# An order written out by hand for the vector engines in an attention pass, with folding ahead of the normalisation

## The chip, the cores and the metric

One NeuronCore of a Trainium2 chip runs the whole program. The metric is the device time of one execution, in microseconds (us). The engines are named as in the profile: PE (TensorE; PEld is its loading of weights), ACT (ScalarE), DVE (VectorE), POOL (GpSimd) and SP (SyncE, which here only issues DMAs). Each takes its instructions in order; semaphores order them between engines.

## The reference, cut to what matters

```python
# x: (1, 2048, 640); two layers, the same weights in both
for layer in range(2):
    n = layernorm(x)
    a, b = n @ hid_re.T, n @ hid_im.T               # 640-point DFT along the channels
    x = x + (seq_re @ a - seq_im @ b)               # real part of the 2048-point DFT
    q, k, v = split_heads(layernorm(x) @ wqkv)      # 32 heads of 20 channels
    pq, pk = phi(q), phi(k)                         # phi(t) = where(t > 0, t + 1, exp(t)) + 1e-6
    kv, z = pk.T @ v, pk.sum(rows)                  # per head
    den = (pq * z).sum(channels of the head) + 1e-6
    x = x + ((pq @ kv) / den) @ wo
```

## The kernel before

The 2048 rows of x stay in SBUF as 16 tiles of 128 rows and 640 channels (X). A product in fp32 is made from two parts of each operand: a high part, rounded by ACT to TensorE's short type (fp32r), and a low part, the rest, subtracted by DVE. Three matmuls (high x high, high x low, low x high) make one product; a few are made in plain fp32, where an instruction of 512 columns counts as two in the profile.

**The attention's second pass** is the function `outputs`. M = kv times wo stands ready in five chunks (rows of M are patched into each other by small transfers). For each row tile n: POOL multiplies phi(q) by z (`weigh`, L444) three tiles ahead; DVE (`weighted`) sums this per head into denominators (L457), adds 1e-6 (L458), takes reciprocals (L459) and multiplies phi(q) by them, 600 columns (L461) and 40 columns (L467), two tiles ahead; PE transposes the weighted tile n+1 in five parts (L140); ACT and DVE split the transposed tile (L134, L135); PE multiplies it by M in 30 matmuls (L168); DVE adds the result to X[n] (L500, the residual). PSUM holds four tiles of 1024 columns, shared by transposes and products.

**Layer 1's folds** run beside it in layer 0. The 2048-point DFT uses symmetries: the channels of a normalised tile are folded (column c with column 640 - c, a sum and a difference), and the tiles of a quad a, b, c, d (tiles 4g to 4g+3) are added and subtracted: a += d, b += c, then a - b, the class "o" (odd rows), and a + b, from which classes "+" and "-" (even rows) come. Class `Fold` holds a row of stages that the loop moves on by one at each step (`tick`). For a finished tile: two passes of ACT for mean and variance (L112, L113), three small instructions of POOL (L114, L115, L118), the normalisation on ACT (L126), the channel folds on POOL (L748, L749, L753), the quad's additions on DVE and POOL (L765, L766, L774, L791), then the even ones (L808 to L812). Tiles 0 to 12 go through this (`PUSHED = 13`). The last three go through a script, the string `SECOND`, whose words each stand for one operation and its engine, followed by the rest of the folds and the splitting of DFT rows that arrive by DMA.

**What sets the order.** In `outputs` a scheduler orders each engine's instructions, with offsets by name (`AHEAD`). In the script, DVE, ACT and POOL run as written. SP's order is always as written, PE's always the scheduler's. A gate delays the script's first DMAs: they wait for the residual of tile `NT - GATE`, with NT = 16.

**After it** PE makes the class products, groups of three column blocks (L902; "cw" are plain fp32 DFT rows, "ch" and "cl" split ones), ACT and DVE split the results u (L927, L928), and the hidden DFT (L947) goes from u to the rows of x.

Of the kernel before, what the change touches and what calls it, by code (L numbers as in the profile page):

```python
# [8 lines left out]
F32 = mybir.dt.float32  # L9
F32R = mybir.dt.float32r  # L10
# [25 lines left out]
SECOND = 'w02a sda x02d x12d x03d x13d x23a sev nea dev sfv nfa dfp nda kep kdp fdp fep x32a v02v ffv kfv y23v ddv y32v a3v x22a y22v b3p c3v h3a x33a w01a v01v y33v x10a y10v l3v t3p p1v m1p P1a w00a w10a w11a v10v u20v v11v u30v u21v u22v u31v x00d x01d M1a v00p w12a v12p x11a u32v y11p Q1p N1p'  # L36
PUSHED = 13
# [5 lines left out]
PAIRS = (1, 0, 0, 0)  # L43
EVENS = (1, 1, 1, 1)
FOLDS = (0, 0)
VLOWS = (0, 0, 1, 0)
WLOWS = ((5, 2), (1, 1))
GATE = 2
# [3 lines left out]
class K:  # L52
    def __init__(self, tc, ctx):
# [10 lines left out]
        nc.vector.memset(self.mhalf, -0.5)  # L64

# [107 lines left out]
class Attention:  # L173
# [273 lines left out]
    def weighted(self, n, t1):  # L447
# [6 lines left out]
        den, rden = (  # L454
            k.sm.tile([128, H], F32, tag="sm" + n, name=k.nm(n), bufs=2) for n in ("den", "rden")
        )
# [16 lines left out]
        return t1  # L473

    def outputs(self, after, between=lambda: None):
# [4 lines left out]
        for n, i in enumerate(self.order2):  # L480
# [16 lines left out]
            for pu, hs in zip(pus, parts):  # L497
                of = lambda t: t[:, hs[0] : hs[-1] + 1, :]
                with k.ahead("res", n):
                    last = nc.vector.tensor_tensor(of(h2(X[i])), of(h2(X[i])), of(halves(pu)), op=ALU.add)  # L500
                after(i, hs[0], hs[-1] + 1)
            if n == NT - GATE:
                late = last
        return late
# [46 lines left out]
class Fold:  # L551
# [5 lines left out]
    def __init__(self, k, X, scalar):  # L557
        self.k, self.X, self.scalar, self.out, self.whole = k, X, scalar, {}, False
        self.stages = [
            self.even_low, self.even, self.odd_low, self.combine, self.pairs, self.fold, self.norm, self.stats  # L560
        ]
        self.queue = {f: [] for f in self.stages}
        self.ab, self.E, self.high, self.abcd = {}, {}, {}, {}

    def push(self, i):
        self.queue[self.stats].append((i, None))

    def tick(self):
        for n, f in enumerate(self.stages):
            todo, self.queue[f] = self.queue[f][:1], self.queue[f][1:]  # L570
            for i, v in todo:
                with self.k.ahead(f.__name__, i):
                    r = f(i, v)
                if r is not None:
                    self.queue[self.stages[n - 1]].append(r)

    def drain(self):
        while any(self.queue.values()):
            self.tick()
# [8 lines left out]
    def script(self, order, four, raws):  # L588
# [14 lines left out]
        for kind, i, c, e in order:  # L603
# [7 lines left out]
            elif kind == "s":  # L611
                xn[i] = k.temp()
                norm.setdefault(g, {})[q] = k.stats(self.X[i], xn[i] if e == "a" else None)
            elif kind == "r":
                norm[g] = self.scales(mv[g], 4 - tail[g], [i - 4 * g for i in onact if i // 4 == g])
            elif kind == "n":
                if self.whole:
                    xn[i] = k.temp()
                else:
                    self.abcd[i] = k.pqp.tile([128, D], F32, tag="pq", name=k.nm("ab"))  # L620
                k.norm(self.X[i], xn[i], norm[g][q])
            elif kind == "f":
                eng.tensor_tensor(self.abcd[i][:, 1:HD], xn[i][:, 1:HD], xn[i][:, HC:], op=ALU.add)  # L623
            elif kind == "d":
# [108 lines left out]
    def stats(self, i, _):  # L733
        k, x = self.k, self.X[i]
        xn = k.temp()
        return i, (xn, k.stats(x, xn if i in self.scalar else None))

    def norm(self, i, v):
        xn, st = v
        self.k.norm(self.X[i], xn, st)  # L740
        return i, xn

    def fold(self, i, xn):
        k, nc = self.k, self.k.nc
        ab = k.pqp.tile([128, D], F32, tag="pq", name=k.nm("ab"))
        g, q = divmod(i, 4)
        eng = nc.gpsimd if i in self.scalar else nc.vector
        eng.tensor_tensor(ab[:, 1:HD], xn[:, 1:HD], xn[:, HC:], op=ALU.add)  # L748
        nc.gpsimd.tensor_copy(ab[:, 0:HC:HD], xn[:, 0:HC:HD])  # L749
        lo, hi = xn[:, 1:HD], xn[:, HC:]  # L750
        if q % 2:
            lo, hi = hi, lo
        nc.gpsimd.tensor_tensor(ab[:, HC:], lo, hi, op=ALU.subtract)  # L753
        self.ab[i] = ab
        if all(4 * g + r in self.ab for r in range(4)):
            return g, [self.ab.pop(4 * g + r) for r in range(4)]

    def pairs(self, g, abcd):
        k, nc = self.k, self.k.nc
        a, b, c, d = abcd  # L760
        eo0 = None
        if g == 0:
            eo0 = k.temp(shape=(1, HC))
            nc.vector.tensor_tensor(eo0, a[0:1, :HC], d[0:1, :HC], op=ALU.subtract)
        nc.vector.tensor_tensor(a, a, d, op=ALU.add)  # L765
        k.engine(PAIRS[g]).tensor_tensor(b, b, c, op=ALU.add)  # L766
        return g, (a, b, c, d, eo0)

    def combine(self, g, v):
        k, nc = self.k, self.k.nc  # L770
        a, b, c, d, eo0 = v
        if g == 0:
            nc.vector.memset(a[0:1, HC:], 0.0)
        nc.vector.tensor_tensor(c, a, b, op=ALU.subtract)  # L774
        self.total(g, a, b, d)
        if g == 0:
            nc.scalar.copy(a[0:1, :HC], c[0:1, :HC])
            nc.vector.tensor_copy(c[0:1, :HC], eo0)
            nc.vector.memset(d[0:1, HC:], 0.0)
        plain = k.plain(2, g)  # L780
        if plain:
            self.out["o", g] = (c,)
        else:
            self.odd_high(g, c)
        self.E[g] = a, b, d
        if g % 2:
            self.queue[self.even].append((g // 2, [self.E.pop(h) for h in (g - 1, g)]))
        return None if plain else (g, (c, self.high[g]))

    def total(self, g, a, b, d):  # L790
        self.k.engine(EVENS[g]).tensor_tensor(d, a, b, op=ALU.add)  # L791

# [9 lines left out]

    def even(self, j, v):
        k, nc = self.k, self.k.nc
        (em, _, d0), (p, _, d1) = v
        if j == 0:
            k.special_row(d1)
            nc.vector.memset(d1[0:1, :HC], 0.0)  # L808
        k.engine(FOLDS[j]).tensor_tensor(p, d0, d1, op=ALU.add)
        nc.vector.tensor_tensor(d0, d0, d1, op=ALU.subtract)  # L810
        if j == 0:
            nc.scalar.copy(d0[0:1, :HC], em[0:1, :HC])  # L812
        if k.plain(0, j):
# [544 lines left out]
```

## Time and profile before

| | |
|---|---|
| median of 3 runs | 805.05 us (804.66 to 805.65) |
| the profiled execution | 805.39 us |
| its span, first to last instruction | 803.5 us, mean TensorE clock 0.992 |
| layer 0's second pass, on PE | 335.64 to 422.60 us of the span |
| the class products of layer 1 after it | 424.14 to 447 us |

Times in the profile count from the span's start. A row of the timeline has start, length, engine, line, operation and tiles, and in brackets the idle time just before it and the instruction that ended it. Lines are those of the kernel before. In a name such as `ps_3553` the number is that of the tile in the program.

### The profile page before, as it was taken

The numbers are of one execution on the slowest core, as the hardware profiler recorded it, in microseconds if no ns is written. First come the engines' busy times: TensorE is split into PE (matmuls) and PEld (weight loads), VectorE is DVE, ScalarE is ACT, GpSimd is POOL, SyncE is SP. The second block draws the span as 40 slices with busy tenths as digits, with TensorE's granted clock in tenths as the row PEclk, the third lists the DMA queues.
The fourth block names the chain that finished last, engine by engine and source line by source line (L and its number), as shares of the span: only waits on it lengthen the run. The fifth ranks groups of instructions, "written<-read, shape, count | busy, mean of one in ns | idle before, by whom it ended". The sixth has DMA issues, their size and how long they took to land.

```text
span 803.5 us, 12981 instructions
## 1 busy us (share of the span) xinstructions
PE 744.2 (93%) x4920; PEld 706.5 (88%) x4920; DVE 612.6 (76%) x1153; ACT 337.7 (42%) x592; POOL 317.7 (40%) x354
## 2 busy tenths in 40 slices
PE   0579999999999999999898999999999999999997
PEld 0138899999999999899784899999999999989997
DVE  7799883778774775989978787377896398499982
ACT  4534544545324553455552434445532455341110
POOL 4987991111021111369894756111101111134310
PEclk9989999999999999999999999999999999999999
DMA  9122430455770452000004551044444044001121
GB/s 329 57 86 66 134 101 1 143 162 175 215 229 15 153 179 78 21 1 2 0 1 145 202 204 48 1 142 142 142 142 141 1 142 144 20 12 50 66 84 70
DMA packets 36008, 81.25 MB, mean 101 GB/s; under 512 B 4142, under 2 KB 5937, under 8 KB 35936
## 3 DMA queue, kind: packets, MB, share of 16 engines
q1 hardware_dynamic: 35904, 80.27, 30.9%
q8 instruction: 41, 0.67, 0.3%
q14 instruction: 31, 0.25, 0.1%
q0 software_dynamic: 32, 0.06, 0.0%
HBM read 68.10 MB, written 11.80 MB: 99 GB/s over the span
## 4 chain that ended last, share of the span: by engine, by line
PE 64%; DVE 21%; POOL 5%; DMA 3%; ACT 3%; issue 3%; SPq 0%; DVEq 0%; POOLq 0%; ACTq 0%
PE ps L168 44%; PE ps L252 13%; PE ps L140 3%; PE ps L947 3%; DVE w L135 2%; DVE t L135 2%; DVE junk L1064 1%; DMA ck<-in_ck 1%; DVE x L974 1%; DVE den L457 1%; POOL ab L623 1%; DVE t L461 1%; PE ps L400 1%; DMA rawc<-in_so 1%; DMA x<-in_x 1%
## 5 line engine op out<-in xcount | busy, mean ns | idle before, releaser
L168 PE MATMUL ps<-w,t 128*128 128x320 f32 x2880 | 440.2, 311 | 7.7 <-DVE t L135 5.7
L168 PEld LDWEIGHTS ps<-w,t 128*128 128x128 f32 x2880 | 422.8, 188 | 10.9 <-DVE t L135 7.7
L299 POOL TENSOR_TENSOR t<-t,s 128x640 f32<-128x640 f32 x32 | 58.3, 1822 | 219.3 <-DVE s L287 211.8
L252 PE MATMUL ps<-t,t 128*128 128x256 f32 (+1 forms) x640 | 139.9, 309 | 0.0
L284 ACT ACTIVATE t<-ps 128x640 f32<-128x640 f32 x64 | 45.2, 705 | 156.3 <-PE ps L168 156.3
L252 PEld LDWEIGHTS ps<-t,t 128*128 128x128 f32 x640 | 107.3, 188 | 0.0
L1064 DVE CUSTOM_DVE_ANT_0 junk<-ck,ck 128x688 bf16<-128x688 f32 (+4 forms) x138 | 98.6, 714 | 7.3 <-DMA ck<-in_ck 5.5
L252 PE MATMUL ps<-w,t 128*128 128x384 f32 (+1 forms) x320 | 98.7, 310 | 0.7 <-DVE w L135 0.6
L444 POOL TENSOR_TENSOR t<-pq,t 128x640 f32<-128x640 f32 x32 | 56.1, 1758 | 101.3 <-ACT t L370 48.5
L135 DVE TENSOR_TENSOR t<-ps,t 128x640 fp32r<-128x640 f32 (+1 forms) x66 | 53.8, 817 | 41.3 <-ACT t L134 41.0
L134 ACT CAST t<-ps 128x640 fp32r<-128x640 f32 (+1 forms) x66 | 45.6, 692 | 67.3 <-PE ps L140 63.1
L902 PE MATMUL ps<-cw,ab 128*107 128x512 f32 (+4 forms) x108 | 42.8, 533 | 33.0 <-DVE ab L643 26.1
L287 DVE SCALAR_TENSOR_TENSOR pq<-t,pq 128x640 f32<-128x640 f32 x32 | 27.6, 861 | 54.3 <-ACT t L286 54.3
L902 PEld LDWEIGHTS ps<-cw,ab 128*107 128x107 f32 (+1 forms) x108 | 18.5, 183 | 51.8 <-issue 47.7
L252 PEld LDWEIGHTS ps<-w,t 128*128 128x128 f32 x320 | 60.1, 188 | 1.5 <-DVE w L135 1.5
L947 PE MATMUL ps<-t,u 107*128 107x322 f32 (+1 forms) x306 | 48.9, 315 | 2.6 <-DVE t L135 1.4
L947 PEld LDWEIGHTS ps<-t,u 107*128 107x128 f32 (+1 forms) x306 | 45.8, 189 | 5.0 <-DVE u L928 2.2
L286 ACT ACTIVATE t<-t 128x640 f32<-128x640 f32 x64 | 48.0, 750 | 0.0
L140 PE MATMUL ps<-ident,t 128*128 128x128 f32 x320 | 45.6, 273 | 1.5 <-DVE t L467 1.0
L128 DVE TENSOR_SCALAR t<-x,kept 128x640 f32<-128x640 f32 x58 | 44.4, 766 | 0.7 <-PE ps L252 0.7
L140 PEld LDWEIGHTS ps<-ident,t 128*128 128x128 f32 x320 | 38.3, 140 | 3.2 <-issue 1.5
L134 ACT CAST t<-t 128x640 fp32r<-128x640 f32 x32 | 23.3, 729 | 36.6 <-DVE t L128 31.8
(178 smaller groups left out, 999.4 us busy)
## 6 DMA issues: line engine op xcount, KB each, us to landing
ck<-in_ck SPq DMA_DIRECT2D x48, 346.0 KB
ck<-in_ck SPq DMA_DIRECT2D x48, 344.0 KB
save<-w SPq DMA_DIRECT2D x20, 320.0 KB
w<-save SPq DMA_DIRECT2D x20, 320.0 KB
x<-in_x SPq DMA_DIRECT2D x16, 320.0 KB
out<-x SPq DMA_DIRECT2D x15, 320.0 KB
raw<-in_wqkv SPq DMA_DIRECT2D x10, 320.0 KB
s<-in_wqkv SPq DMA_DIRECT2D x10, 320.0 KB
```

Of the source, the lines that this page charges most:

```text
L134: self.nc.scalar.copy(hi, src)
L135: self.engine(pool).tensor_tensor(lo, src, hi.bitcast(F32), op=ALU.subtract)
L140: self.nc.tensor.transpose(tp[:, 128 * c : 128 * c + 128], src[:, 128 * c : 128 * c + 128], self.ident)
L168: nc.tensor.matmul(pu[:m, 512 * h : 512 * h + HD], s, w[:, HD * h : HD * h + HD], start=first, stop=last)
L252: nc.tensor.matmul(self.place(G, c, part), x[:, 128 * c : 128 * c + 128], p[:, f : f + n], start=start and i == 0, stop=stop and i == 2, s ...
L284: nc.scalar.activation(h2(e), halves(pu), AF.Relu, scale=-1.0)
L286: nc.scalar.activation(e, e, AF.Exp, scale=-1.0)
L299: nc.gpsimd.tensor_tensor(pksum, pksum, pk, op=ALU.add)
L444: k.nc.gpsimd.tensor_tensor(t1, self.PQ[self.order2[n]], self.zb, op=ALU.mult)
L902: nc.tensor.matmul(pu[:m, o : o + n], e, w[:, f : f + n], start=g == 0 and i == 0, stop=g == end and not more and i == len(both) - 1,)
L947: self.k.nc.tensor.matmul(po[:, o : o + 322], s[:m, f : f + 128], w[:m, x, :], start=first, stop=last)
L1064: i = nc.vector.tensor_tensor_reduce(k.junk[:, : a.shape[1]], b, a, 1.0, 0.0, op0, op1, o)
```

## The change

- **The order.** For layer 0 a new function `outputs_by_hand` writes the loop with the folds in it, and DVE, ACT and POOL run in the order as written, there and in the script. Per step: POOL weighs tile n+4; DVE adds the residual of n-1, makes the low part of n+1, and then one weighted tile, from step 3 on (`LEAD`) that of n+3 instead of n+2, two of them in step 3; ACT makes the high part of n+1, then the statistics of n-1; POOL folds tile n-1. A quad's operations come at fixed steps.
- **Folding first.** POOL folds x itself (L821, L825), not the normalised tile; two unpaired columns are doubled by ACT (L814). ACT then scales and shifts the folded tile in two halves (L810, L811), only for two tiles of a quad (three in the first); the other two get their scale within DVE's addition (L841). What this leaves out by a factor of two is made up in the hidden DFT's weights (`twice`).
- **Normalisation by quads.** The small instructions of POOL work on a quad's four tiles at once (`scales2`, L796 to L802). All 16 tiles' statistics are made by ACT (before, two of the last tiles' by DVE).
- **Denominators in PSUM.** `weighted` puts denominators and reciprocals into free columns of the transposes' PSUM tile (layer 0 alone): L459 to L461 work in place there, L463 and L469 read them from there.
- **The gate** is the residual of tile 12 (step 13's first operation on DVE); before, of tile 14.
- `SECOND` is a new list, now for tiles 12 to 15's remaining folds and the same DFT rows. It begins

```diff
-SECOND = 'w02a sda x02d x12d x03d x13d x23a sev nea dev sfv nfa dfp ...
+SECOND = 'x02d x03d x12d x13d x22a x23a sfa ffv dfp kfa c2v r3p h2a ...
```

Behind the hidden products of layer 1 all engines' instructions stand in the same order before and after.

On DVE at the start of the pass (L135 and L134 are low parts, `w` those of M, `t` those of a tile; `x` is a residual). Before:

```order
L135 TENSOR_TENSOR w_3486<-ps_3478,w_3485 120x640
L457 TENSOR_REDUCE den_3553<-t_3543 128x32
L135 TENSOR_TENSOR w_3499<-ps_3491,w_3498 120x640
L457 TENSOR_REDUCE den_3604<-t_3545 128x32
L135 TENSOR_TENSOR w_3512<-ps_3504,w_3511 120x640
L458 TENSOR_SCALAR den_3553<-den_3553 128x32
L135 TENSOR_TENSOR w_3525<-ps_3517,w_3524 120x640
L458 TENSOR_SCALAR den_3604<-den_3604 128x32
L135 TENSOR_TENSOR w_3538<-ps_3530,w_3537 120x640
L135 TENSOR_TENSOR t_3592<-ps_3547,t_3591 128x640
```

and after:

```order
L134 TENSOR_TENSOR w_3488<-ps_3480,w_3487 120x640
L134 TENSOR_TENSOR w_3501<-ps_3493,w_3500 120x640
L134 TENSOR_TENSOR w_3514<-ps_3506,w_3513 120x640
L134 TENSOR_TENSOR w_3527<-ps_3519,w_3526 120x640
L134 TENSOR_TENSOR w_3540<-ps_3532,w_3539 120x640
L134 TENSOR_TENSOR t_3591<-ps_3553,t_3590 128x640
L459 TENSOR_REDUCE ps_3553<-t_3545 128x32
L460 TENSOR_SCALAR ps_3553<-ps_3553 128x32
L461 RECIPROCAL ps_3553<-ps_3553 128x32
```

The denominators' first operations moved behind all low parts. On DVE in the middle of the pass, two steps of the loop (`ab` are folded tiles). Before:

```order
L500 TENSOR_TENSOR x_113<-x_113,ps_4054 128x640
L458 TENSOR_SCALAR den_4181<-den_4181 128x32
L461 TENSOR_TENSOR t_4039<-pq_1101,rden_4118 128x5x120
L467 TENSOR_TENSOR t_4039<-pq_1101,rden_4118 128x2x5x4
L459 RECIPROCAL rden_4182<-den_4181 128x32
L461 TENSOR_TENSOR t_4109<-pq_1198,rden_4182 128x5x120
L467 TENSOR_TENSOR t_4109<-pq_1198,rden_4182 128x2x5x4
L766 TENSOR_TENSOR ab_4091<-ab_4091,ab_4155 128x640
L135 TENSOR_TENSOR t_4169<-ps_4111,t_4168 128x640
L500 TENSOR_TENSOR x_115<-x_115,ps_4124 128x640
L765 TENSOR_TENSOR ab_4021<-ab_4021,ab_4219 128x640
```

and after:

```order
L485 TENSOR_TENSOR x_113<-x_113,ps_3968 128x640
L134 TENSOR_TENSOR t_4057<-ps_4018,t_4056 128x640
L459 TENSOR_REDUCE ps_4018<-t_3959 128x32
L460 TENSOR_SCALAR ps_4018<-ps_4018 128x32
L461 RECIPROCAL ps_4018<-ps_4018 128x32
L463 TENSOR_TENSOR t_3959<-pq_1103,ps_4018 128x5x120
L469 TENSOR_TENSOR t_3959<-pq_1103,ps_4018 128x2x5x4
L848 TENSOR_TENSOR ab_3759<-ab_3647,ab_3703 128x640
L852 COPY ab_3759<-t_3955 1x321
L853 MEMSET ab_3820 1x319
L485 TENSOR_TENSOR x_115<-x_115,ps_4025 128x640
```

The low part now stands right behind the residual, and the folds' additions behind the weighted tile. On POOL at the same place, before:

```order
L444 TENSOR_TENSOR t_4109<-pq_1198,t_3280 128x640
L115 TENSOR_TENSOR mv_4027<-ve_4028,mhalf 128x1
L114 TENSOR_SCALAR ve_4098<-mv_4097 128x1
L118 TENSOR_TENSOR mv_4027<-mv_4027 128x1
L115 TENSOR_TENSOR mv_4097<-ve_4098,mhalf 128x1
L118 TENSOR_TENSOR mv_4097<-mv_4097 128x1
L748 TENSOR_TENSOR ab_4155<-t_4026 128x319
L749 COPY ab_4155<-t_4026 128x2
L753 TENSOR_TENSOR ab_4155<-t_4026 128x319
```

and after:

```order
L849 TENSOR_TENSOR ab_3820<-ab_3647,ab_3703 128x640
L796 TENSOR_SCALAR qve_4077<-qmv_3880 128x4
L800 TENSOR_TENSOR qrs_4078<-qve_4077,mhalf 128x4
L801 TENSOR_TENSOR qmv_3880<-qmv_3880,qrs_4078 128x4
L802 TENSOR_TENSOR qbo_4079<-qmv_3880 128x2
L443 TENSOR_TENSOR t_4084<-pq_1624,t_3282 128x640
L821 TENSOR_TENSOR ab_4132<-x_115 128x319
L825 TENSOR_TENSOR ab_4132<-x_115 128x319
```

The three small instructions of each tile became four of each quad, ahead of the weighing. The diff, cut:

```diff
-GATE = 2
+GATE = 3
+LEAD = 3
-    def weighted(self, n, t1):
+    def weighted(self, n, t1, ps=None):
...
+        if ps is not None:
+            den, rden = ps[:, :H], ps[:, H:]
...
+    def outputs_by_hand(self, T):
+        k, nc, X = self.k, self.k.nc, self.X
+        q, wt, t1 = self.first, {1: self.next}, {2: self.t1}
+        pu = late = None
+        def residual(n, pu, hs):
+            of = lambda t: t[:, hs[0] : hs[-1] + 1, :]
+            return nc.vector.tensor_tensor(of(h2(X[n])), of(h2(X[n])), of(halves(pu)), op=ALU.add)
+        for n in range(NT):
+            if n % 4 == 1 and 4 < n < 14:
+                T.scales2(n // 4 - 1)
+            for m in (3, 4) if n == 0 else (n + 4,):
+                if m < NT:
+                    t1[m] = self.weigh(m)
+            if n + 1 < NT:
+                tp = k.transposed(wt.pop(n + 1))
+            if n:
+                last = residual(n - 1, pu, range(2))
+                if n == NT - GATE:
+                    late = last
+            parts = [range(2)] if n + 1 < NT else [(0,), (1,)]
+            pus = [k.psum() for _ in parts]
+            for pu, hs in zip(pus, parts):
+                product(nc, pu, *q, [m[0] for m in self.M], [m[1] for m in self.M], hs)
+            if n + 1 < NT:
+                q = k.split_chunks(tp)
+            if n:
+                T.fold(n - 1)
+            if n % 4 == 1 and 4 < n < 14:
+                T.normed(n // 4 - 1)
+            for u, m in enumerate((n + 2,) if n < LEAD else (n + 2, n + 3) if n == LEAD else (n + 3,)):
+                if m < NT:
+                    wt[m] = self.weighted(m, t1.pop(m), tp[:, D + 2 * H * u :][:, : 2 * H])
+            T.tick(n)
+        for pu, hs in zip(pus, parts):
+            residual(n, pu, hs)
+        return late
...
+    def norm2(self, g, q, ab):
+        nc, c = self.k.nc, COL[q]
+        rs, mv, both = self.scale[g]
+        shift = mv[:, c, 1:2] if g == 0 and q in (0, 3) else both[:, c - 2 : c - 1]
+        nc.scalar.activation(ab[:, :HC], ab[:, :HC], AF.Identity, bias=shift, scale=rs[:, c : c + 1])
+        nc.scalar.activation(ab[:, HC:], ab[:, HC:], AF.Identity, scale=rs[:, c : c + 1])
...
+    def added(self, g, q, to, other):
...
+            nc.vector.scalar_tensor_tensor(
+                to, to, self.scale[g][0][:, q : q + 1], other, op0=ALU.mult, op1=ALU.add
+            )
```

More of the change, by code (lines that the diff above doesn't have):

```diff
@@ L64, in __init__ @@
         nc.vector.memset(self.mhalf, -0.5)
+        self.two = self.cst.tile([128, 2], F32, name="two")
+        nc.vector.tensor_scalar(self.two, self.ident[:, 0:DC:DC - 1], -1.0, 2.0, op0=ALU.mult, op1=ALU.add)
     def nm(self, s):
@@ L499, in outputs @@
                 with k.ahead("res", n):
-                    last = nc.vector.tensor_tensor(of(h2(X[i])), of(h2(X[i])), of(halves(pu)), op=ALU.add)
+                    nc.vector.tensor_tensor(of(h2(X[i])), of(h2(X[i])), of(halves(pu)), op=ALU.add)
                 after(i, hs[0], hs[-1] + 1)
-            if n == NT - GATE:
-                late = last
-        return late
 def layer_fourier_general(k, X, crt, cit, wrt, wit):
@@ L551, with __init__, tick @@
 class Fold:
[L557 to L579, printed above, removed]
+    def __init__(self, k, X):
+        self.k, self.X, self.out, self.whole = k, X, {}, False
+        self.ab, self.E, self.high, self.abcd, self.mv, self.scale = {}, {}, {}, {}, {}, {}
+    def tick(self, n):
+        for g in range(3):
+            stage = n - 4 * g - 6
+            if stage in (0, 1):
+                a, b, c, d = (self.ab[4 * g + r] for r in range(4))
+                self.added(g, stage, *((b, c) if stage else (a, d)))
+            elif stage == 2 and g < 2:
+                self.combine(g)
+        if 13 <= n:
+            (self.even_row, self.even_sum, self.even_rest)[n - 13]()
     def begin(self):
@@ L628, in script @@
                 eng.tensor_tensor(self.abcd[i][:, HC:], lo, hi, op=ALU.subtract)
+            elif kind == "k" and not self.whole:
+                self.unmirrored(self.X[i], self.abcd[i])
             elif kind == "k":
@@ L633, in script @@
                 eng.tensor_tensor(self.em, a[0:1, :HC], d[0:1, :HC], op=ALU.subtract)
+            elif kind in "ab" and not self.whole:
+                self.added(g, *((0, a, d) if kind == "a" else (1, b, c2)))
             elif kind == "a":
@@ L769, in combine, with normed @@
[L769 to L773, printed above, removed]
+        self.unmirrored(x, ab)
+    def normed(self, g):
+        for q in (0, 3, 2) if g == 0 else (3, 2):
+            self.norm2(g, q, self.ab[4 * g + q])
+    def added(self, g, q, to, other):
+        nc, k = self.k.nc, self.k
+        if g == 0 and q == 0:
+            self.em = k.temp(shape=(1, HC))
+            nc.vector.tensor_tensor(self.em, to[0:1, :HC], other[0:1, :HC], op=ALU.subtract)
+            nc.vector.tensor_tensor(to, to, other, op=ALU.add)
+            nc.vector.memset(to[0:1, HC:], 0.0)
+        else:
+            nc.vector.scalar_tensor_tensor(
+                to, to, self.scale[g][0][:, q : q + 1], other, op0=ALU.mult, op1=ALU.add
+            )
@@ L781, in combine, with even_row @@
[L781 to L784, printed above, removed]
-        self.E[g] = a, b, d
[L786 to L791, printed above, removed]
+        assert k.plain(2, g)
+        self.out["o", g] = (c,)
+        self.E[g] = a, b, d
+    def even_row(self):
+        d1 = self.E[1][2]
+        self.k.special_row(d1)
+        self.k.nc.vector.memset(d1[0:1, :HC], 0.0)
@@ L1172, in fast_path @@
         k.layer, k.part = 1, 2 * layer + 1
-        T = Fold(k, X, range(NT - 1))
+        T = Fold(k, X)
         if layer == 0:
-            after, between = (lambda i, a, b: i < PUSHED and T.push(i)), T.tick
+            with k.tc.manual_schedule(engines=three):
+                four.gate = att.outputs_by_hand(T)
+                four.open()
+                T.script(SECOND, four, {})
         else:
             k.ends, flags = check.ends, []
-            after, between = store, lambda: flags or flags.append(verdict(k))
-        gate = att.outputs(after, between)
-        if layer == 0:
-            T.drain()
-            four.open()
-            four.gate = gate
-            with k.tc.manual_schedule(engines=three):
-                T.script(SECOND, four, {})
+            att.outputs(store, lambda: flags or flags.append(verdict(k)))
     assert not check.now and not check.pieces
```

149 lines of the change are left out of this document (76 added, 73 removed).

## The prediction

> **What bounds the kernel now.** I read the engines' shares first, then TensorE's rows in order of time through the stage that is edited, then what ends its idle time there, then the busy time of the other engines in that stretch. In the first part of the page, columns are busy us and share of the span:
>
> ```profile
> PE 744.2 (93%) x4920; PEld 706.5 (88%) x4920; DVE 612.6 (76%) x1153; ACT 337.7 (42%) x592; POOL 317.7 (40%) x354
> ```
>
> PE is the bound as a mean, so only time in which PE waits can be won. PE's rows in layer 0's second pass (start, length; in brackets the idle time before a row and what ended it):
>
> ```profile
> 335.64 4.66 PE L168 MATMUL ps<-w,t 128*128 128x320 f32 x30 [0.63 <-DVE w L135]
> 340.40 0.73 PE L140 MATMUL ps<-ident,t 128*128 128x128 f32 x5
> ...
> 375.05 0.71 PE L140 MATMUL ps<-ident,t 128*128 128x128 f32 x5
> ...
> 389.50 4.08 PE L168 MATMUL ps<-w,t 128*128 128x320 f32 x26 [2.11 <-DVE t L135]
> ...
> 414.12 8.48 PE L168 MATMUL ps<-w,t 128*128 128x320 f32 x56 [0.91 <-DVE t L135]
> ```
>
> Between 340.40 and 375.05 seven steps pass, 34.65 us, so 4.95 us is a step in which PE never waits. Step 0 takes 4.76 (335.64 to 340.40), fourteen more steps 69.3, the last product 4.66: without a stall the pass would end at 335.64 + 4.76 + 69.3 + 4.66 = 414.36. It ends at 414.12 + 8.48 = 422.60. So **8.25 us** are lost, all after 375. The windows of 40 us tell who is full there (columns: us, busy time of PE, PEld, DVE, ACT, POOL, then clock):
>
> ```profile
> 340.00:380.00 40.00, 39.04 (x276) 38.49 (x275) 35.93 (x60) 22.73 (x46) 32.06 (x44) 1.00 0.00 1
> 380.00:420.00 40.00, 34.81 (x233) 32.77 (x233) 35.30 (x50) 22.05 (x44) 36.45 (x49) 1.00 0.00 1
> ```
>
> POOL has 36.45 of 40 and DVE 35.30; ACT has slack, and the clock is full. The chain that ended last walks from POOL over DVE into PE there:
>
> ```profile
> 411.00 0.82 POOL ab L753
> 411.85 1.48 DVE ab L766
> 413.33 0.74 DVE t L135
> ```
>
> A fold on POOL releases an add of layer 1 on DVE, which stands ahead of the low part that PE waits for. The stage is held by two engines that are too full, and by what their queues put first.
>
> **POOL.** One tile's work on POOL, in a quiet stretch:
>
> ```profile
> 344.93 0.19 POOL L114 TENSOR_SCALAR ve<-mv 128x1 f32<-128x1 f32 x1 [5.43 <-ACT t L113]
> 345.20 0.55 POOL L115 TENSOR_TENSOR mv<-ve,mhalf 128x1 f32<-128x1 f32 x1
> 345.83 0.19 POOL L118 TENSOR_TENSOR mv<-mv 128x1 f32<-128x1 f32 x1
> 345.99 1.57 POOL L444 TENSOR_TENSOR t<-pq,t 128x640 f32<-128x640 f32 x1
> 348.74 0.89 POOL L748 TENSOR_TENSOR ab<-t 128x319 f32<-128x319 f32 x1 [1.19 <-ACT t L126]
> 349.57 0.19 POOL L749 COPY ab<-t 128x2 f32<-128x2 f32 x1
> 349.72 0.88 POOL L753 TENSOR_TENSOR ab<-t 128x319 f32<-128x319 f32 x1
> ```
>
> Together 4.46 us; four tiles and one whole-row add (L791, the shape of L444, 1.57) make 19.4 of the 19.8 us of four steps. Afterwards a tile costs 1.57 + 0.89 + 0.88 = 3.34, and a quad has four small instructions, 0.19 + 0.55 + 0.19 + 0.19 = 1.12: 13.4 + 1.57 + 1.12 = 16.1 of 19.8. POOL stops being a bound. Its folds also no longer wait for ACT's norm (the 1.19 above), as they read x itself.
>
> **DVE.** Five rows in a stretch where POOL rests (its row of 344.93 shows 5.43 us of idle time before it), and the means over the whole pass (busy us, mean ns, idle before):
>
> ```profile
> 340.91 0.77 DVE L461 TENSOR_TENSOR t<-pq,rden 128x600 f32<-128x600 f32 x1
> 341.60 0.19 DVE L467 TENSOR_TENSOR t<-pq,rden 128x40 f32<-128x40 f32 x1
> 341.71 0.81 DVE L500 TENSOR_TENSOR x<-x,ps 128x640 f32<-128x640 f32 x1
> 342.44 0.17 DVE L458 TENSOR_SCALAR den<-den 128x32 f32<-128x32 f32 x1
> 342.64 0.35 DVE L459 RECIPROCAL rden<-den 128x32 f32<-128x32 f32 x1
> ```
>
> ```profile
> L461 DVE TENSOR_TENSOR t<-pq,rden 128x600 f32<-128x600 f32 x14 | 16.0, 1143 | 0.2
> L135 DVE TENSOR_TENSOR t<-ps,t 128x640 fp32r<-128x640 f32 x14 | 11.4, 814 | 0.5 <-ACT t L134 0.3
> L457 DVE TENSOR_REDUCE den<-t 128x32 f32<-128x640 f32 x12 | 9.7, 809 | 0.6 <-POOL t L444 0.6
> L467 DVE TENSOR_TENSOR t<-pq,rden 128x40 f32<-128x40 f32 x14 | 6.6, 469 | 0.0
> L458 DVE TENSOR_SCALAR den<-den 128x32 f32<-128x32 f32 x12 | 4.9, 405 | 0.1
> L774 DVE TENSOR_TENSOR ab<-ab,ab 128x640 f32<-128x640 f32 x3 | 3.7, 1224 | 0.0
> ```
>
> The same L461 is 0.77 or, on average, 1.143; L467 0.19 or 0.469; L458 0.17 or 0.405: 0.37 + 0.28 + 0.235 = 0.89 us a step are lost beside POOL. The operations with PSUM as a source or one big source (L135 at 0.814 on average, L500 at 0.81) show no such stretch. With the denominators in PSUM, L461 and L467 read one operand from SBUF and one from PSUM, the form of L500, so I take the quiet prices: a step is 0.81 (L500) + 0.81 (L135) + 0.80 (L457, less its overlap) + 0.17 + 0.35 + 0.77 + 0.19 = 3.90. No row shows a reduction into PSUM or a 32-column operation on it; the ends are the quiet rows (3.90) and the means of now (4.79), and L500 and L135, nearest in form, speak for the first. A rule of the Trainium skill lies behind the same row: its page SBUF — State Buffer, in the section on the two separate sides, says that a DVE operation with two SBUF inputs and a GpSimd operation exclude each other for a whole instruction. L461's 1.143 agrees for two SBUF inputs, L500's 0.81 for one; by it the 3.90 holds and the folds' adds stay exposed.
>
> The folds add to DVE two L841 and one L848 per quad, in place of two or three adds, two SBUF sources, so I take L774's 1.224 each (ends 0.8, the quiet form, and twice 0.8): 3.7 a quad. A quad is then 4 x 3.90 + 3.7 = 19.3 of 19.8. It fits, barely, and the adds fall unevenly (the first quad's in steps 6 to 8, all with small row copies). A weighted tile is ready a step earlier from step 3 on, so a lag of some 3 us of DVE reaches PE only partly. I keep **1.0 us** of the 8.25 as a stall that stays; ends 0 (it fits) and 3 (all adds at 1.6, about 1 us over per quad).
>
> **ACT.** Four half-row normalisations a quad (six in the first), against four of these whole ones:
>
> ```profile
> L126 ACT ACTIVATE t<-x,mv 128x640 f32<-128x640 f32 x13 | 11.8, 919 | 13.0 <-POOL mv L118 13.0
> ```
>
> By the share of columns a half is 0.46, so four to six are 1.8 to 2.8 where 3.7 stood, now in one burst behind the statistics; were a half as dear as a whole they are 3.7 to 5.5. ACT has 22.05 of 40 busy; the high part (L134) of step 6 and 10 may come about 1 us late. The low part is due a step ahead of its product, which hides that, so I cost it at nothing; if that cover is gone it costs 1 us twice.
>
> **The first step.** DVE's rows ahead of the first product:
>
> ```profile
> 332.60 0.80 DVE L457 TENSOR_REDUCE den<-t 128x32 f32<-128x640 f32 x1
> ...
> 334.06 0.80 DVE L457 TENSOR_REDUCE den<-t 128x32 f32<-128x640 f32 x1
> ```
>
> Two reductions, 1.6 us, stand between M's low parts, on one of which the product at 335.64 waits. The given order puts them behind. M's high parts on ACT and its row transfers then limit: I take **1.0** of at most 1.6 (at least 0). In exchange, steps 1 and 2 have one chain without much slack: transposes 0.7, high part 0.7, low part 0.81, the reduction to L467 2.29, that is 4.5 of 4.95.
>
> **The loads and the adds.** Rows of DVE, SP and PE at the pass's end:
>
> ```profile
> 419.28 1.31 DVE L800 TENSOR_TENSOR tl<-ab,th 128x640 fp32r<-128x640 f32 x1 [2.01 <-ACT th L795]
> 420.51 0.81 DVE L500 TENSOR_TENSOR x<-x,ps 128x640 f32<-128x640 f32 x1
> 421.34 0.83 SPq L847 DMA_DIRECT2D cw<-in_co  x2
> 424.14 2.80 PE L902 MATMUL ps<-cw,ab 128*107 128x512 f32 x6 [1.53 <-DMA cw<-in_co]
> 427.74 7.97 PE L902 MATMUL ps<-cw,ab 128*107 128x512 f32 x18 [0.80 <-DMA cw<-in_so]
> 442.03 0.95 PE L902 MATMUL ps<-ch,tl 128*107 128x512 f32 x3 [0.75 <-DVE tl L800]
> 447.16 8.31 PE L947 MATMUL ps<-t,u 107*128 107x322 f32 x54 [0.98 <-DVE u L928]
> ```
>
> The gate, tile 14's residual, ran at 420.51 behind L800, which itself waited 2.01 us for ACT; SP issued at 421.34, 1.3 us before PE was done, and PE waited 1.53 and 0.80 for the transfers. Gated by tile 12's residual at the head of step 13 they start some 14 us ahead, and 2.8 us was all that the first needed: 2.33 go. The 0.75 before the last group goes if tile 15's chain is shorter: a half residual 0.4, two passes of ACT for its statistics (two of L126, 1.9), POOL 1.1, the norms of two tiles 1.9, three DVE operations 3.7, a split 1.6, some of it side by side: 10 to 12 us behind the pass's end. PE has the 24 fp32 instructions before it, 2.80 + 7.97 = 10.8 us, and the third group's 18 products; it did 24 of that kind between 435.71 and 441.28, 0.23 each, so 4.2 more, 15.0 in all. So **3.08** go; at worst 2.3. Behind it stand the halves of u, ACT and DVE in turn: 0.98 now; with the adds closer together and the hidden weights' scaled subtracts (L935) still among them I expect **0.5** more, between 0.98 less and 1 more.
>
> **The sum.** 8.25 - 1.0 + 1.0 + 3.08 - 0.5 = 10.83 us. After the hidden products the rows on all engines stand in the same order as before, so nothing there moves but in time. The profiled execution took 805.39 (span 803.5), 0.34 over the median of 805.05: 805.39 - 10.83 = 794.56, as a median **794.2**.
>
> **Rivals.** (1) POOL and DVE still stretch each other: a DVE step is 4.79, a quad 4 x 4.79 + 3.7 = 22.9 against 19.8, 3 us over in the two full quads; 6 us of the 8.25 stay instead of 1: 799.2. For it speaks that DVE had 35.30 of 40 and gains no slack but these 0.89 a step; against it L500's 0.81 in the same pass. (2) Small operations on PSUM are dearer: L460 and L461 take twice what L458 and L459 take now, 0.52 a step; a quad is 4 x 4.42 + 3.7 = 21.4, 1.6 over in about three quads, 4 us more than I keep: 798. No row shows a 32-column operation on PSUM; against it stands that 640 columns cost the same from PSUM (L500, 0.81) as the reduction costs from SBUF (0.80). The Trainium skill speaks for this one: its page Perfetto Trace Analysis, Optimizing Scalar/DVE Operations, gives DVE's overhead on PSUM as about 125 ns against 60 on SBUF. By that page five operations cost 0.33 a step more, an estimate of 2 us in all and of 796 for the time; no row here shows the 65 ns. (3) Slower: DVE's line is now fixed, so whatever is late in it holds the low part behind it. L463 reads its reciprocals from PSUM, each repeated over 20 columns, and no row shows that. If a step averaged 4.95 + 10.83/15 = 5.67, the gain would be gone: 0.84 above 4.83, the mean step of a quad, which L463 at 1.6 in place of 0.77 would do. At 2.0 the steps are 1.1 too long, 16.7 us against 10.8: 811. Against it, the same repeated pattern costs 0.77 from SBUF. (4) The waits only move: uneven adds keep 5 to 6 us in the pass, and tile 15's chain or u takes what the loads give, so that less than 1.6 is left: 804. Against it, the 3 us of cover before the last group.
>
> **Chances.** The sum with its bounds (791 to 797) 0.58; rival 1 (797 to 802) 0.15; rival 2 (796 to 799) 0.10; rival 3 0.07; rival 4 0.05; better than all bounds 0.05. The best bounds together give 1.0 + 0.6 + 1.5 more than the sum, 791; the range reaches from there into rival 1, 791 to 801.5. A measurement of this kernel tells 0.2%, 1.6 us, from no change: faster 0.88, same 0.05, slower 0.07.
>
> **What would show it.** Right: the pass's transposes 4.95 apart to the end and its end near 414; SP's first class load about 14 us ahead of the last product; no wait for cw; L463 near 0.8 and L469 near 0.2 beside busy POOL; POOL near 80% in the pass. Wrong: L463 above 1.1 or small PSUM rows above 0.4; waits of PE for L134's DVE rows in steps 6 to 13; a new wait for u of over 2 us.

## The result, and the profile after

The changed kernel takes 797.56 us (median of 4 runs, 797.4 to 798.84) against 804.88 (804.66 to 805.65) of the kernel before, run beside it: ratio 0.9911, 95% interval 0.9894 to 0.9928, so 7.3 us less, with 5.8 to 8.5 in the interval. The prediction was 794.2, 791 to 801.5. The profiled execution of the changed kernel took 798.84 (span 797.0), at the top of its runs.

PE's timeline after the change, the same places as in the prediction (start, length; in brackets the idle time before and what ended it):

```profile
335.98 4.65 PE L167 MATMUL ps<-w,t 128*128 128x320 f32 x30
340.75 0.74 PE L139 MATMUL ps<-ident,t 128*128 128x128 f32 x5
...
405.20 0.71 PE L139 MATMUL ps<-ident,t 128*128 128x128 f32 x5
405.66 9.02 PE L167 MATMUL ps<-w,t 128*128 128x320 f32 x60
414.52 10.46 PE L968 MATMUL ps<-cw,ab 128*107 128x512 f32 x24
...
434.55 1.09 PE L968 MATMUL ps<-cw,ab 128*107 128x258 f32 x4 [1.24 <-DMA cw<-in_ce]
...
436.88 0.41 PE L1013 MATMUL ps<-t,u 107*128 107x322 f32 x1 [1.01 <-DVE u L994]
439.69 0.63 PE L1013 MATMUL ps<-t,u 107*128 107x322 f32 x1 [2.39 <-DVE u L994]
...
473.75 7.19 PE L167 MATMUL ps<-w,t 128*128 128x320 f32 x48
```

and two rows of the kernel before, for the last two marks of the table below:

```profile
444.90 1.03 PE L902 MATMUL ps<-cw,ab 128*107 128x258 f32 x4
...
480.56 7.22 PE L168 MATMUL ps<-w,t 128*128 128x320 f32 x48
```

Thirteen steps from 340.75 to 405.20 are 64.45 us, 4.96 each: the pass has no stall left. Behind the class products of the odd rows PE now waits 1.24 us for a load and 1.01 and 2.39 us for u. I split the stretch at five marks: the start of the products for M (x60), the pass's first product, the pass's end, the end of the class products of the odd rows (where the next product follows without a wait, the start of that one, which the profile sets 0.16 us earlier), and layer 1's first product of 128 x 320 behind the hidden DFT:

| us, from the timelines | to the first product | the pass | odd class products | to layer 1's first product |
|---|---|---|---|---|
| before | 14.76 | 86.96 | 22.30 | 35.66 |
| after | 14.67 | 78.70 | 18.63 | 40.44 |
| gained | 0.09 | 8.26 | 3.67 | -4.78 |

That is 7.24. What is left to the 6.5 between the two spans lies outside (0.43 ahead of the first mark, 0.31 behind the last); where those 0.7 us come from is not shown.

The windows show who became lighter (columns as before: us, PE, PEld, DVE, ACT, POOL, clock):

```profile
340.00:380.00 40.00, 39.88 (x282) 39.41 (x281) 34.00 (x63) 22.27 (x52) 25.54 (x27) 1.00 0.00 1
380.00:414.00 34.00, 34.00 (x242) 33.96 (x241) 28.07 (x50) 21.51 (x52) 23.82 (x27) 1.00 0.18 60
```

POOL has 70% of 380 to 414 where it had 91% of 380 to 420, DVE 83% where it had 88%. DVE's groups in the pass (busy us, mean ns, idle before):

```profile
L463 DVE TENSOR_TENSOR t<-pq,ps 128x600 f32<-128x600 f32 x14 | 10.9, 778 | 0.5
L841 DVE SCALAR_TENSOR_TENSOR ab<-ab,qrs,ab 128x640 f32<-128x640 f32 x5 | 4.5, 899 | 0.0
L469 DVE TENSOR_TENSOR t<-pq,ps 128x40 f32<-128x40 f32 x14 | 2.6, 189 | 0.0
L460 DVE TENSOR_SCALAR ps<-ps 128x32 f32<-128x32 f32 x13 | 2.6, 199 | 0.5
```

L463 at 0.778 stands where L461 had 1.143, L469 at 0.189 for 0.469, L460 at 0.199 for 0.405: the quiet prices, beside a POOL that is still busy most of the time. (L458, now L460, has only one source, so the contention of two operands in SBUF does not cover it; that it is dearer in SBUF beside POOL is shown, why is not.) The new places of the loads and of the late ones, on SP:

```profile
403.43 0.37 SPq L901 DMA_DIRECT2D cw<-in_co  x1
...
418.80 0.33 SPq L894 DMA_DIRECT2D rawc<-in_so  x1
419.41 0.33 SPq L921 DMA_DIRECT2D rawh<-in_wr  x1
427.59 0.33 SPq L894 DMA_DIRECT2D rawc<-in_ce  x1
...
430.25 0.42 SPq L901 DMA_DIRECT2D cw<-in_ce  x1
```

The first class goes out 11 us ahead of the pass's end. But the line then stops twice ahead of `cw<-in_ce`, for 12 and 8 us, because rows to be split need a staging buffer (`raw`, four of them) that DVE frees, and `cw<-in_ce`, which needs none, stands behind them.

### The profile page after: what moved, and what is told of

Its sections match the earlier page's. It is cut to its first block, busy times and chain, and to the rows that moved or that the text cites. A ratio compares the mean times of both kernels' runs of the same rounds, so it can differ in the third digit from the quotient of the medians.

```text
span 797.0 us, 12963 instructions
## 1 busy us (share of the span) xinstructions
PE 742.1 (93%) x4920; PEld 708.7 (89%) x4920; DVE 600.7 (75%) x1148; ACT 343.1 (43%) x620; POOL 294.2 (37%) x306
## 4 chain that ended last, share of the span: by engine, by line
PE 66%; DVE 21%; POOL 4%; ACT 4%; issue 2%; DMA 2%; SPq 0%; DVEq 0%; POOLq 0%; ACTq 0%
PE ps L167 42%; PE ps L251 15%; PE ps L1013 4%; PE ps L139 3%; DVE w L134 2%; DVE t L134 2%; PE ps L968 1%; DVE t L463 1%; DVE x L485 1%; POOL ab L659 1%; DVE ps L459 1%; DVE junk L1130 1%; PE ps L399 1%; DMA x<-in_x 1%; DVE ab L841 1%
## 5 line engine op out<-in xcount | busy, mean ns | idle before, releaser
L134 DVE TENSOR_TENSOR t<-ps,t 128x640 fp32r<-128x640 f32 (+1 forms) x66 | 53.9, 818 | 46.5 <-ACT t L133 46.4
L1013 PE MATMUL ps<-t,u 107*128 107x322 f32 (+1 forms) x306 | 51.4, 328 | 7.0 <-DVE u L994 5.6
L1013 PEld LDWEIGHTS ps<-t,u 107*128 107x128 f32 (+1 forms) x306 | 49.0, 202 | 8.6 <-DVE u L994 6.3
```

The source lines that it names most:

```text
L134: self.engine(pool).tensor_tensor(lo, src, hi.bitcast(F32), op=ALU.subtract)
L1013: self.k.nc.tensor.matmul(po[:, o : o + 322], s[:m, f : f + 128], w[:m, x, :], start=first, stop=last)
```

## The experiments

All were timed beside the kernel before, whose median was 804.5 to 804.7 us there; times are medians, in brackets the ratio to the kernel before and its 95% interval. The changed kernel's 797.56 is from a batch of its own, so a difference to it of under 2 us is not clear of noise. Figures of single stages come from one profiled execution each. My theory was: the pass is freed by DVE's quiet prices together with a lighter POOL, and what was lost behind it is the queue of late loads. The rivals: the order alone, POOL alone, or (behind the pass) the alternation of ACT and DVE on u.

**e3, denominators back in SBUF.**

```diff
-                    wt[m] = self.weighted(m, t1.pop(m), tp[:, D + 2 * H * u :][:, : 2 * H])
+                    wt[m] = self.weighted(m, t1.pop(m))
```

> The changed kernel with the denominators back in SBUF, nothing else. If DVE's operations with two SBUF inputs are stretched beside POOL as in the kernel before (0.89 us a step), the multiplication by the reciprocals is again above 1.0 us on average, a step of DVE is about 4.8 and PE waits for low parts in steps 6 to 13: 2 to 5 us slower than the changed kernel, 799.5 to 802.5. If the given order and the lighter POOL are what freed the pass, under 1 us slower: 797.3 to 798.5.

805.03 us (ratio to before 1.0007, 0.9998 to 1.0016): the whole gain is gone. The pass takes 85.16 us instead of 78.70, and the three operations are stretched again:

```profile
L463 DVE TENSOR_TENSOR t<-pq,rden 128x600 f32<-128x600 f32 x13 | 15.2, 1172 | 0.5
L460 DVE TENSOR_SCALAR den<-den 128x32 f32<-128x32 f32 x13 | 7.0, 538 | 0.4
L469 DVE TENSOR_TENSOR t<-pq,rden 128x40 f32<-128x40 f32 x13 | 5.2, 404 | 0.0
```

The operations' form and order are otherwise the same, so it is the place of the denominators and reciprocals that decides: 0.39 + 0.34 + 0.22 = 0.95 us a step. I had expected 2 to 5 us; it is 7.5, of which 6.5 lie in the pass. PE's waits there, none of which the changed kernel has:

```profile
PE ps L167 <- DVE x L485: 1.6, 2, 1.2
PE ps L139 <- DVE t L469: 1.5, 4, 0.6
PE ps L167 <- ACT t L133: 0.6, 1, 0.6
PE ps L167 <- DVE t L134: 0.2, 1, 0.2
```

**e10, only the denominators in PSUM, in the kernel before.**

```diff
-                    wt = self.weighted(n + 2, t1)
+                    wt = self.weighted(n + 2, t1, tp[:, D : D + 2 * H] if k.part == 1 else None)
```

> The kernel before with only the denominators of layer 0 in PSUM, under the scheduler and with the old folds. If DVE's stretched operations alone made the 8.25 us of stalls, most go: 797.5 to 800. If POOL, at 97% of a step, holds the pass as well, about half: 800 to 803. If only the order counts: 804 to 805.5.

804.35 (0.9996, 0.9982 to 1.001): nothing. The quiet prices are there (its L464, the multiplication, has 776 ns), and DVE's busy time from 340 to 420 falls from 71.2 to 63.3 us, yet the pass takes 89.93 us. The scheduler orders this kernel anew, and PE waits for high parts too (2.3 us, on ACT). After two groups of waits the clock falls as well:

```profile
391.41 6.35 PE L168 MATMUL ps<-w,t 128*128 128x320 f32 x30 [1.09 <-ACT t L134]
```

30 matmuls of 4.65 us take 6.35. So cheap operations on DVE are needed (e3) and not enough (e10). What is missing here can be POOL's load or the order that the scheduler found; the next runs take them apart.

**e13, a full POOL in the changed kernel.** `fold` issues a tile's first fold twice into the same place:

```diff
+        nc.gpsimd.tensor_tensor(ab[:, 1:HD], x[:, 1:HD], x[:, HC:], op=ALU.add)
         nc.gpsimd.tensor_tensor(ab[:, 1:HD], x[:, 1:HD], x[:, HC:], op=ALU.add)
```

> The changed kernel with each tile's first fold on POOL done twice (0.9 us more a step, so 19.6 of the 19.8 us of four steps, as much as POOL had before); the result is the same. If a full POOL alone brings back stalls although DVE no longer shares with it, 2 to 6 us slower than the changed kernel's 797.6: 799.6 to 803.6. If DVE's stretched operations are the only reason and POOL's load no matter, under 1 us slower: 797.2 to 798.6.

802.32 (0.9974, 0.9962 to 0.9985): 4.8 slower than the changed kernel, 4.0 of it in the pass (82.70). POOL is busy for 28.70 us of 380 to 414, 84%, where the changed kernel has 70%. Its groups and its PE waits in the pass:

```profile
L463 DVE TENSOR_TENSOR t<-pq,ps 128x600 f32<-128x600 f32 x13 | 10.1, 778 | 0.4
L842 DVE SCALAR_TENSOR_TENSOR ab<-ab,qrs,ab 128x640 f32<-128x640 f32 x4 | 4.7, 1184 | 0.0
L849 DVE TENSOR_TENSOR ab<-ab,ab 128x640 f32<-128x640 f32 x2 | 3.6, 1806 | 0.0
```

```profile
PE ps L167 <- DVE x L485: 1.6, 1, 1.6
PE ps L167 <- ACT t L133: 0.7, 1, 0.7
PE ps L167 <- DVE t L134: 0.2, 1, 0.2
```

L463 stays at 778 ns. What comes back are late chains. Ahead of the wait of 1.6, ACT stands 3.12 us for POOL (2.18 in the changed kernel), whose sum comes later, and DVE's one-row copy waits for ACT in front of the residual; ahead of the wait of 0.7, a stretched addition on DVE delays a residual, and with it ACT's statistics, norms and high part. The folds' additions, with both operands in SBUF, are stretched from 868 to 1806 ns (L849, in the changed kernel L848). So POOL's lighter load is a cause beside the denominators' place; as DVE still shares with POOL in the additions, the run does not part POOL's own lateness from that.

**e7, the scheduler's order in the pass.** The loop stands outside the block in which DVE, ACT and POOL run as written:

```diff
-            with k.tc.manual_schedule(engines=three):
-                four.gate = att.outputs_by_hand(T)
-                four.open()
+            four.gate = att.outputs_by_hand(T)
+            four.open()
+            with k.tc.manual_schedule(engines=three):
```

> The changed kernel's operations and program text, but the scheduler and not the text orders ACT, DVE and POOL within the pass (the script behind it stays by hand). If the operations (POOL lighter, PSUM denominators) free the pass, the same within 1 us: 797 to 798.5. If the order by hand is what frees it, waits for low parts come back: 2 to 5 us slower, 799.5 to 802.5.

798.08 (0.9931, 0.9918 to 0.9943): not to be told from the changed kernel by time. In the trace the pass takes 80.73 us, 2.0 more, and the rest 2.4 less (38.05 in the last column): `cw<-in_ce` goes out as early after the pass's start as in the changed kernel (94.4 against 94.3 us), so the wait for it is gone, and the first wait for u is 0.25 instead of 1.01. Given the operations, the order by hand is worth some 2 us in the pass, and nothing in the time while the stretch behind the pass waits. The pass of e10 was the scheduler's too and took 89.93 us, so what e10 lacked was chiefly the lighter folds.

**e6, no lead.**

```diff
-LEAD = 3
+LEAD = 16
```

> The changed kernel without the step of lead: the weighted tile stays two tiles ahead through the whole pass. If the lead is what absorbs the folds' additions (my reading of the lag), transposes wait for them in steps 6 to 13, 1 to 3 us slower than the changed kernel's 797.6: 798.6 to 800.6. If a step of DVE of 3.9 us fits without it, the same: 797.2 to 798.2.

798.47 (0.9933, 0.9919 to 0.9947), between the two expected ranges and not to be told from the changed kernel by time; the pass takes 80.67, again 2.0 more, with these waits, the only ones in it:

```profile
PE ps L139 <- DVE t L469: 0.9, 2, 0.6
PE ps L139 <- POOL t L443: 0.5, 1, 0.5
```

In the pass the lead absorbs the folds' additions, as the prediction had it: without it PE waits for the weighted tile in three steps. Behind the pass the waits shrink as in e7.

**e9 and e4, the gate.** In the kernel before it is moved to tile 12, in the changed one back to tile 14:

```diff
-GATE = 2
+GATE = 4
```

> The kernel before with only the gate moved from tile 14's residual to tile 12's. Its waits for cw (2.3 us at the adds' start) go if buffers are free by then: 801.5 to 803.5. After the run with the late gate (4.3 us slower than the changed kernel) it may be more, 800.5; if other engines' lateness replaces the wait, 804 to 805.

```diff
-GATE = 3
+GATE = 1
```

> The gate of the first loads is the residual of tile 14 again, now at the head of step 15. If the earlier loads are worth what the old waits were (2.3 us at PE), 1 to 3 us slower than the changed kernel: 798.5 to 800.5, with waits for cw at the adds' start or later ones for staging buffers. If the new order of DVE alone (residual ahead of everything in a step) already brings this gate early enough, the same within 0.5: 797 to 798.

In the kernel before the early gate gives 804.26 (1.0002, 0.9993 to 1.0011), nothing by time: the odd class products take 21.09 instead of 22.30, the waits for cw are gone, and the waits for tile 15's class (tl, th) are 2.1 us where 0.75 stood. In the changed kernel the late gate costs 4.3 us: 801.87 (0.9961, 0.9947 to 0.9976); more than the 1 to 3 expected. PE waits 1.7 us at the first class product and, since the staging buffers turn over later, 2.4 for `cw<-in_ce` where it waited 1.24. So the early gate is worth more with the new order than with the old one.

**e1, the even rows' loads first.** In `SECOND` the words `x00d x01d` move behind `x13d`.

> The two loads of the even rows (cw<-in_ce, cw<-in_se) are issued straight behind the other whole classes, ahead of the loads that wait for a staging buffer. Theory A (behind the pass the time is lost to loads queued on SP behind waits for staging buffers, and these late loads also hold up ACT, so u comes late): the 1.24 us wait for cw<-in_ce goes, but the hidden rows still come late and PE then waits for u instead: 0 to 1.2 us faster than the changed kernel's 797.6, that is 796.4 to 797.6. Theory B (u is late because its ACT and DVE halves alternate, whatever the loads do): the wait is merely exchanged for one on u, 797.3 to 797.8.

797.38 (0.9911, 0.9896 to 0.9926). The wait for cw is gone and the two for u are 1.11 and 2.39, as in the changed kernel: the one wait mattered little while u is late.

**e2, staging buffers freed early.**

```diff
-... l2v nfa nea w02a x32a a3v b3v c3v h3a t3p y32v x33a l3v w01a y33v v02v v01v x10a ...
+... l2v w02a x32a v02v y32v nfa nea x33a w01a a3v b3v c3v h3a t3p y33v v01v l3v x10a ...
```

> ACT and DVE treat the already loaded hidden rows and the class rows that free staging buffers before they wait for tile 15's normalisation. Theory A: SP's loads behind the buffers start 3 to 5 us earlier, the wait for cw<-in_ce goes, the waits for u fall from 3.4 to under 1.5 us, the clock does not drop near 440; 3 to 4.5 us faster than the changed kernel: 793 to 794.6. Theory B: the cw wait goes, u still waits over 2.5 us: 796.5 to 797.5.

795.91 (0.9893, 0.9878 to 0.9908), 1.6 less than the changed kernel, and its interval overlaps that one's. `rawc<-in_ce` goes out at 419.92 instead of 427.59, the wait for cw is gone, the first for u is 0.25; the second is still 2.39. Theory A was half right: the last two columns lose 1.0 us with the loads (58.1 us from the pass's end instead of 59.1), and most of the wait for u is not theirs. The time fell between the two expected ranges.

**e11, the hidden weights ahead of u.** As e2, and:

```diff
-... w11a u20v u30v v10v v11v u21v u31v u22v x00d x01d M1a v00v w12a ...
+... w11a v00v v10v v11v u20v u30v u21v u31v u22v x00d x01d M1a w12a ...
```

> The run with the staging buffers freed early (e2_raw_free, 795.9 us), and in it the hidden weights' low parts ahead of all halves of u on DVE, u in the order of its PSUM tiles. In e2 PE still waited 2.4 us at the hidden product's second PSUM tile, which is free only when u's second tile is read. Theory A' (u's halves stand behind the scaled subtracts in DVE's line): that wait falls to about 1.4 us, 0.9 us off, and up to 1 us more if PE then keeps its full clock in the next 5 us (it had 0.59 there): 794 to 795.2. Theory B (the alternation of ACT and DVE sets it): 795.5 to 796.3.

794.28 (0.9879, 0.9865 to 0.9893), the fastest here, 3.3 less than the changed kernel. PE's timeline, and 2 us windows of it and of the changed kernel (the clock is the third column from the right):

```profile
434.31 1.15 PE L1013 MATMUL ps<-t,u 107*128 107x322 f32 x6 [1.55 <-DVE u L994]
436.07 3.84 PE L1013 MATMUL ps<-t,u 107*128 107x322 f32 x24 [0.60 <-ACT u L993]
```

```profile
436.00:438.00 2.00, 1.93 (x13) 1.94 (x14) 1.25 (x3) 2.00 (x5) 0.00 (x0) 1.00 1.01 389
438.00:440.00 2.00, 2.00 (x16) 2.00 (x16) 2.00 (x3) 0.01 (x1) 1.58 (x3) 1.00 1.01 401
```

```profile
436.00:438.00 2.00, 0.41 (x1) 0.19 (x1) 1.86 (x4) 0.59 (x2) 0.00 (x0) 0.88 0.00 0
438.00:440.00 2.00, 0.32 (x1) 0.32 (x2) 1.29 (x3) 1.68 (x4) 0.00 (x0) 0.50 0.85 271
440.00:442.00 2.00, 2.00 (x9) 2.00 (x9) 1.72 (x4) 1.38 (x4) 0.54 (x1) 0.50 0.89 270
442.00:444.00 2.00, 2.00 (x9) 2.00 (x9) 1.81 (x2) 0.00 (x0) 1.02 (x3) 0.50 0.99 334
444.00:446.00 2.00, 2.00 (x14) 2.00 (x13) 0.00 (x0) 0.00 (x0) 0.00 (x0) 0.92 1.00 393
```

The first fence is e11's timeline, the second its windows, the third the changed kernel's. In the changed kernel PE works 0.73 us of 436 to 440, the clock is granted at 0.50 from about 437.5 to 444.3 (worked out from the means of the windows), and PE does 18 matmuls in 440 to 444 where it would do 28 and more. In e11 PE waits 1.55 and 0.60 and keeps its clock. So the changed kernel's waits cost twice: once as idle time and once as about 2 us at half the clock (two windows of 2 us at 0.50). In e2, where the first wait is short but the second is 2.39, the clock falls too (0.73 and 0.59 as means of 435 to 440 and 440 to 445). Between e2 and e11 the waits for u shrink by 0.5 us only (2.64 to 2.15), the last column by 2.9: most of what e11 gains is the clock. That holds for the profiled executions; e11's four times are 793.0 and 793.4 at mean clocks of 0.993 and 0.994, and 795.2 and 795.5 at 0.988 and 0.990, so the clock may well fall in some of its executions, which no trace here shows.

**e12, POOL held back ahead of the pass.** As e11, and the weighing of tile 4 on POOL waits for the last 120x120 low part on DVE:

```diff
+        if k.part == 1 and n == 4:
+            k.after(r, k.lo120)
```

> As e11_u_row, and POOL's weighing of tile 4 waits until DVE's last 120x120 low part is done. If that weighing, a POOL operation of 1.6 us with SBUF operands, is what held these low parts (2.48 us for two, 1.12 in the kernel before), PE's waits of 0.69 and 0.18 ahead of the first product go and the pass starts 0.9 to 1.3 us earlier than in e11_u_row. If something else holds them, no difference (within 0.4).

794.36 (0.9879, 0.9865 to 0.9893), no different by time. The timelines of DVE and POOL show what was expected; the first two fences are the changed kernel (DVE, then POOL), the other two e12:

```profile
331.25 2.48 DVE L134 TENSOR_TENSOR w<-t,w 120x120 fp32r<-120x120 f32 x2
333.65 3.73 DVE L134 TENSOR_TENSOR w<-ps,w 120x640 fp32r<-120x640 f32 x5
```

```profile
327.70 5.89 POOL L443 TENSOR_TENSOR t<-pq,t 128x640 f32<-128x640 f32 x3 [5.73 <-PE ps L399]
```

```profile
330.99 1.11 DVE L134 TENSOR_TENSOR w<-t,w 120x120 fp32r<-120x120 f32 x2
332.02 3.87 DVE L134 TENSOR_TENSOR w<-ps,w 120x640 fp32r<-120x640 f32 x5
```

```profile
332.18 3.10 POOL L445 TENSOR_TENSOR t<-pq,t 128x640 f32<-128x640 f32 x2 [0.41 <-DVE w L134]
```

The kernel before, DVE and POOL at the same place:

```profile
330.82 1.12 DVE L135 TENSOR_TENSOR w<-t,w 120x120 fp32r<-120x120 f32 x2
```

```profile
331.82 1.57 POOL L444 TENSOR_TENSOR t<-pq,t 128x640 f32<-128x640 f32 x1 [0.22 <-DVE w L135]
```

The two small low parts take 1.11 instead of 2.48 (each alone: 0.92 and 0.27 instead of 0.93 and 1.63), and the way to the pass's first product 13.43 us instead of 14.68. In this execution 1.4 us were lost ahead of that mark (it stands at 321.05, in e11 at 319.63), where both kernels are the same; the time can't show the 1.25, the trace does.

## Why the prediction was right, and where not

**The pass (8.25 - 1.0).** Right in cause and too careful in size: 8.26 went, nothing stayed. A DVE step is 0.80 + 0.82 + 0.83 + 0.20 + 0.37 + 0.78 + 0.19 = 3.99 by the groups of the changed kernel, against 3.90 forecast. The additions were the mis-sized term: L841 took 0.90 each, not 1.224. With POOL fuller, in e13, the same additions take 1.18, so POOL's pauses are the likely reason. Rival 1 did not come, but e3 shows that its condition was the right one and its price nearly so: 6.4 us of stalls stay in the pass (85.16 against 78.72 without any), where it had 6. Rivals 2 and 3 fell: the five operations on PSUM cost at most 0.03 us each more than the quiet ones in SBUF, and the repeated read of reciprocals costs nothing. The rule of the Trainium skill quoted there (SBUF — State Buffer, the two separate sides) holds in every run for the multiplication: with two operands in SBUF it takes 0.94 to 1.17 us on average beside POOL, with one in PSUM 0.77 to 0.78. It does not cover L458, which has one source and was stretched too (0.405; L460 0.538 in e3): the prediction counted that row to the same cause, and the cost went with the move, but the cause of it is not shown. The other (Perfetto Trace Analysis, Optimizing Scalar/DVE Operations), 65 ns more on PSUM, is not borne out for L460 (0.20 against 0.17) and L461 (0.37 against 0.35).

**POOL.** The estimate of 16.1 of 19.8 us, near 80%, was high: 23.82 of 34 is 70%. That POOL stops being a bound holds. e13 shows that going back to 84% costs 4.0 us in the pass, which the prediction had not priced by itself.

**ACT at nothing.** Right: no wait for a high part in the pass.

**The first step (+1.0).** Wrong: 0.09. The reductions did move behind the low parts, but POOL's three weighings now follow each other without a pause, and the second of DVE's last two 120x120 low parts, with two operands in SBUF, waits out the third weighing. In the kernel before, that weighing started only behind the low part. e12 restores this and finds 1.25; e10, where the weighing waits as before and one reduction at most stands among the low parts, also has 13.43 us. So the 1.0 was there to be had: the prediction reckoned with the contention in the loop and left it out at the start.

**Loads and adds (+3.08).** Right, a little small: 3.67, no wait for `cw<-in_co` or `cw<-in_so` and none for the last group. The loads went out 11 us ahead of the pass's end, not 14, which was early enough. But the sign "no wait for cw" failed further on: PE waits 1.24 for `cw<-in_ce`, which belongs to the next term.

**The u's (-0.5).** The step that failed: "Behind it stand the halves of u ... I expect 0.5 more". It was 4.78 more, and the prediction's own sign of being wrong, a new wait for u of over 2 us, came (2.39). The waits are 1.24 for a load that I had not looked at and 3.40 for u where 0.98 stood; then the clock took about 2; a wait of 0.86 further on is gone. I took the way from the adds to u as one of durations, while it is one of queues: SP's line stood for staging buffers that DVE frees only behind tile 15's chain, ACT's casts of u stood behind the hidden weights, DVE's halves of u behind their low parts, and PE's next PSUM tile behind u. e2 and e11 take these away one after the other and get back 3.7 of the 4.78 (36.77 us in the last column, about 2 of it the clock). What is left is 1.1, with waits for u of 1.55 and 0.60. There ACT and DVE still wait for each other's halves of u (ACT 2.06 and 0.92 us, DVE 0.65 and 0.71), and no run takes this alternation away, so it stays a possible cause of the rest. Rival 4 named the place, without the mechanism.

**The sum.** 10.83 forecast, 7.24 found between the marks: 1.0 and 0.6 better in the pass and the adds, 0.9 worse at the start, 4.3 worse behind the adds. That 797.56 lies inside the range is in part luck: it lies above the sum's own bounds (791 to 797), in the part that was there for rival 1, which did not come, and two terms that were 1.6 us too careful made up for part of the 5.2 missed in the other two.

## What to carry to other kernels

Where DVE and POOL work side by side, look for DVE's operations with two operands in SBUF: the same row at two prices in one profile shows the contention, and moving one small operand to PSUM took 0.95 us of a step of 4.9 away. By itself that was worth nothing (e10, a pass of 89.93 us); with the lighter folds, and the scheduler's order in both, the pass took 80.73 (e7). When a stage becomes faster, ask of every load behind it which buffer it stands for and who frees that, and put operations that free a buffer ahead of those that wait for a chain. Short waits of PE close together can cost more than their sum, as the clock can fall.

## What the runs showed of the hardware that I had not expected

- TensorE's clock was granted at 0.50 for about 6.8 us, though no single wait was over 2.39 us and PE had worked 1.73 of the 3.4 us before it. In the traces here from 300 to 480 us each such drop lasts 3.4 us (e7, and twice in e10) or 6.8 us (the changed kernel, e1, e2, e3, e4, e6, e13), and PE had worked 0.41 (e1) to 1.80 us (e10) of the 3.4 us before. The kernel before has a wait of 2.11 us, and e11 waits of 1.55 and 0.60 close together, without it. The Trainium skill (TensorE: Matmul & The Clock Gate, Part 1) speaks of a half clock after an idle window of about 3.4 us; the drops here last one or two of these, but the time before them was not idle. Where the limit lies was not measured.
- The reciprocals and reductions on PSUM cost within 0.03 us of what they cost in SBUF (0.366 against 0.35, 0.828 against 0.80).
- A small DVE operation can wait out a whole POOL operation when both its operands lie in SBUF: a 120x120 subtraction that took 0.27 us in e12 took 1.63 beside the third weighing.
